# Retention and SwiGLU block: the FFN products by one level of Strassen, over segments of two sequences

## The chip, the cores and the metric

The kernel runs on one core of a Trainium2 chip. The metric is device time in microseconds (us) of one execution; lower is better. One execution was also recorded by the hardware profiler, and all rows below come from that one.

## What is computed

A recurrent retention layer over four sequences of 768 positions, with eight heads of 64, and then a SwiGLU feed-forward block over all 3072 tokens (the model dimension is 512, the inner one 1536):

```python
for t in range(S):
    state = gamma * state + einsum('bhd,bhe->bhde', k[:, :, t], v[:, :, t])
    y[:, :, t] = scale * einsum('bhd,bhde->bhe', q[:, :, t], state)
x = y.transpose(0, 2, 1, 3).reshape(B * S, H * D)     # 3072 x 512
g = x @ w_gate
out = (g / (1 + exp(-g)) * (x @ w_val)) @ w_out
```

`q`, `k`, `v` are float32. The three weight matrices come as float64; the kernel turns them into float32 on the chip.

## The kernel before

Retention is done in chunks of 128 positions, 24 of them, in three steps: `scores` (L175, masked on VectorE at L180, with `qd` and `kd` made on GpSimd at L185 and L189), `mix` (L226 and L230; ScalarE copies the result into `xT` at L233) and `state` (L202, then VectorE at L208 to L212). A chunk's `mix` needs the state that the chunk before it in its sequence left.

The FFN runs over six tiles of 512 tokens. `up` takes one block of 128 of the 1536 inner columns: four float32 matmuls of 128 x 512 for gate and four for value (L257), the Silu on ScalarE (L261) and the product on VectorE (L263). There are twelve such units in a tile. `down` makes 128 tokens of output in twelve matmuls (L268), copied out by ScalarE (L271) and stored; there are four in a tile. All weights lie in SBUF for the whole run. The order is written out by hand in program order: the retention steps of a tile stand between the units of the tile before, so every engine and queue takes its work in that order.

The weights come in 36 pieces of 128 x 512 float64 (12 of gate, 12 of value, 12 of out). A piece is loaded as raw words by a DMA from SP (L107, four raw buffers, three pieces ahead) and turned into float32 in `convert_piece`: six operations on VectorE (L122 to L131), one on ScalarE (L132) and two on GpSimd (L133, L135). Three pieces are converted after each unit of the first tile, four in the prologue.

Of the kernel before, what the change touches and what calls it, by code (L numbers as in the profile page):

```python
# [10 lines left out]
F32 = mybir.dt.float32  # L11
U32 = mybir.dt.uint32
# [13 lines left out]
NT = B * S // T  # L26

# columns of the table of decays
# [5 lines left out]
def tile_retnet_swiglu(  # L34
    ctx: ExitStack,
    tc: tile.TileContext,
    q_t: bass.AP,        # [chunk, (head of pair, d), pair, position]
    k_t: bass.AP,        # likewise
    k_n: bass.AP,        # [chunk, position, (head, d)]
    v_n: bass.AP,        # likewise  # L40
    decays: bass.AP,     # [P, NTAB]
    w_gate: bass.AP,     # float32, or float64 as the bits of int64
# [15 lines left out]
    loads = ctx.enter_context(tc.tile_pool(name="loads", bufs=4))  # L58
    raws = ctx.enter_context(tc.tile_pool(name="raws", bufs=4))
    mid = ctx.enter_context(tc.tile_pool(name="mid", bufs=2))  # L60
    hp = ctx.enter_context(tc.tile_pool(name="hp", bufs=NF + 2))
    io = ctx.enter_context(tc.tile_pool(name="io", bufs=2))
    psum = ctx.enter_context(
        tc.tile_pool(name="psum", bufs=1, space=bass.MemoryType.PSUM))
    ctx.enter_context(tc.manual_schedule())
# [5 lines left out]
    chunks = {}  # L71

    def load_chunk(c):
        tiles = []
        for nm, src in (("kt", k_t), ("qt", q_t), ("kn", k_n), ("vn", v_n)):
            t = loads.tile([P, 512], F32, tag=nm, name=f"{nm}_{c}")
            nc.sync.dma_start(out=t, in_=src[c])
            tiles.append(t)
        chunks[c] = tiles

    tab = consts.tile([P, NTAB], F32, name="tab")
    load_chunk(0)
    nc.scalar.dma_start(out=tab, in_=decays)
    for c in range(1, CPT):
        load_chunk(c)
    wg = [consts.tile([P, NC, P], F32, name=f"wg{f}") for f in range(NF)]
    wv = [consts.tile([P, NC, P], F32, name=f"wv{f}") for f in range(NF)]
    wo = [consts.tile([P, DM], F32, name=f"wo{f}") for f in range(NF)]
    pieces = []
    for f in range(NF):  # L90
        for w, src in ((wg, w_gate), (wv, w_val)):
            pieces.append((w[f].rearrange("p c f -> p (c f)"),
                           src[:, ts(f, P)].rearrange("(c p) f -> p c f", p=P)))
    for f in range(NF):
        pieces.append((wo[f], w_out[ts(f, P)]))
    landed = {}

    def load_piece(n):
        dst, src = pieces[n]
# [10 lines left out]
    def convert_piece(n):  # L110
        """float64 -> float32, rounded to nearest. The words are (lo, hi); hi holds
        the sign, 11 bits of exponent and 20 of mantissa. hi << 3 without its sign is
        the float32 of those 20 bits but for the top bit of the exponent, which is the
        other way round. hi is first brought into float32's range by its magnitude,
        compared as float32 (the order of the bits): below it becomes 0, above inf."""
        if n not in landed:
            return
        dst = pieces[n][0]
# [3 lines left out]
        nc.vector.tensor_scalar(d, hi, 0x7FFFFFFF, None, op0=ALU.bitwise_and)  # L122
# [8 lines left out]
        nc.vector.tensor_scalar(hi, d, 0xFF800000, None, op0=ALU.bitwise_and)  # L131
        nc.scalar.activation(lo.bitcast(F32), lo, AF.Copy, scale=2.0 ** -52)  # L132
        nc.gpsimd.tensor_tensor(lo.bitcast(F32), lo.bitcast(F32), hi.bitcast(F32),  # L133
                                op=ALU.mult)
        nc.gpsimd.tensor_tensor(dst, dst, lo.bitcast(F32), op=ALU.add)  # L135

    AHEAD = 3              # raw pieces on their way
    n_piece = [0]

    def next_piece():  # L140
        n = n_piece[0]
        if n == len(pieces):
            return
        n_piece[0] += 1
        if n + AHEAD < len(pieces):
            load_piece(n + AHEAD)
        convert_piece(n)

    for n in range(AHEAD):
        load_piece(n)  # L150
# [6 lines left out]
    # two states by turns: a pair's two heads as the diagonal blocks of 128 x 128  # L157
    states = [consts.tile([P, NP, P], F32, name=f"state{i}") for i in range(2)]
    for t in states:
        nc.gpsimd.memset(t, 0.0)  # L160

# [1 line left out]
    xT = {}  # L163
    att = {}

    def pairs(t):
        return t.rearrange("p (n t) -> p n t", n=NP)

    def scores(c):
# [13 lines left out]
        if c % NCK:  # L183
            qd = mid.tile([P, NP, P], F32, tag="qd", name=f"qd_{c}")
            nc.gpsimd.tensor_tensor(qd, qt, qdec, op=ALU.mult)  # L185
            att[c, "qd"] = qd
        if c % NCK < NCK - 1:
            kd = mid.tile([P, H, D], F32, tag="kd", name=f"kd_{c}")
# [5 lines left out]
    def state(c):  # L194
# [9 lines left out]
        new, old = states[c % 2], states[(c + 1) % 2]  # L204
# [10 lines left out]
    def mix(c):  # L215
        ci, t, j = c % NCK, c // CPT, c % CPT
        vn = chunks[c][3]
        a = att.pop(c)
        if j == 0:
            xT[t] = mid.tile([P, NC, T], F32, tag="xT", name=f"xT_{t}")  # L220
        y = bank("y", 1, f"y_{c}")
        if ci:
            qd = att.pop((c, "qd"))
            prev = states[(c + 1) % 2]
# [8 lines left out]
        nc.scalar.copy(xT[t][:, :, ts(j, P)], pairs(y))  # L233

    def retention(t):
# [3 lines left out]
        def last(c):  # L239
            state(c)  # L240
            if c + CPT < B * NCK:
                load_chunk(c + CPT)

        steps = []
        for c in range(CPT * t, CPT * (t + 1)):
            steps += [lambda c=c: scores(c), lambda c=c: mix(c), lambda c=c: last(c)]
        return steps

# [1 line left out]
    hT = {}  # L250

    def up(t, f):
        ps = []
        for w in (wg, wv):
            p_ = bank("mlp", 4, f"up{len(ps)}_{t}_{f}")
            for c in range(NC):
                nc.tensor.matmul(p_, w[f][:, c], xT[t][:, c],  # L257
                                 start=(c == 0), stop=(c == NC - 1))
            ps.append(p_)
        sg = io.tile([P, T], F32, tag="sg", name=f"sg_{t}_{f}")  # L260
        nc.scalar.activation(sg, ps[0], AF.Silu)  # L261
        hT[f] = hp.tile([P, T], F32, tag="h", name=f"h_{t}_{f}")
        nc.vector.tensor_tensor(hT[f], sg, ps[1], op=ALU.mult)  # L263

    def down(t, j):
        o = bank("mlp", 4, f"o_{t}_{j}")
        for f in range(NF):
            nc.tensor.matmul(o, hT[f][:, ts(j, P)], wo[f],  # L268
                             start=(f == 0), stop=(f == NF - 1))
        ev = io.tile([P, DM], F32, tag="ev", name=f"ev_{t}_{j}")  # L270
# [77 lines left out]
```

## Time and profile before

| what | value |
|---|---|
| time, median of three runs (lowest, highest) | 964.25 us (964.19, 964.88) |
| span of the profiled execution, first to last instruction | 962.0 us |
| TensorE busy | 861.0 us, 89% of the span |
| VectorE busy | 258.7 us, 27% |
| GpSimd busy | 135.3 us, 14% |
| ScalarE busy | 95.9 us, 10% |
| mean granted TensorE clock | 0.954 of 2.4 GHz |

The span is 2.25 us under the median of the runs. The rows further down come from views of the trace: stretches of time with the busy time of each engine, the waits by what ended them, the chain of work that ended last, the order in time, and groups of like instructions. PE is TensorE, PEld its weight loads, DVE VectorE, ACT ScalarE, POOL GpSimd, and SP the engine whose queue issues most DMAs. A float32 matmul stands in the trace as two records, and some records are missing.

### The profile page before, as it was taken

The page shows a single profiled execution, that of the slowest core. Times are in us where ns is not written, and L with a number is a line of the kernel's source. Part 1 is how long each engine was busy: PE and PEld are TensorE (multiplying, and loading weights), DVE is VectorE, ACT ScalarE, POOL GpSimd, SP SyncE. Part 2 cuts the span into 40 slices and gives each one's busy share as a digit, 9 for nine tenths or more (in the row PEclk, how much of TensorE's full clock was granted, in tenths as well). Part 3 has the DMA queues.
Part 4 walks back from the last instruction along what each step waited for, and adds up shares of the span by engine and source line. Part 5 has one row for each costly group of instructions (what it writes and reads, how often), then busy time and mean ns, then how long its engine had stood idle before and what let it go on. Part 6 is the DMA issues. An engine that isn't in the chain of part 4 may idle for free.

```text
span 962.0 us, 7015 instructions
## 1 busy us (share of the span) xinstructions
PE 861.0 (89%) x2816; PEld 421.7 (44%) x2816; DVE 258.7 (27%) x408; ACT 95.9 (10%) x158; POOL 135.3 (14%) x118
## 2 busy tenths in 40 slices
PE   4797560629999999999999999999999999999998
PEld 3632220314545544444554544444454444444443
DVE  3789999470111211011121012010021210010100
ACT  1121111100000010000000010000000000000000
POOL 2545555360000000000000000000000000000000
PEclk8799985769999999999999999999999999999999
DMA  8223346322120100110111111011000000000000
GB/s 295 86 69 115 124 154 197 110 87 65 48 74 12 45 33 30 58 44 24 32 38 50 33 44 45 11 44 55 33 1 1 0 1 22 22 1 0 0 12 33
DMA packets 31857, 51.58 MB, mean 54 GB/s; under 512 B 2512, under 2 KB 14800, under 8 KB 31824
## 3 DMA queue, kind: packets, MB, share of 16 engines
q1 hardware_dynamic: 28224, 44.05, 14.3%
q10 hardware_dynamic: 3600, 7.09, 2.1%
q8 instruction: 22, 0.36, 0.2%
q14 instruction: 11, 0.09, 0.0%
HBM read 44.83 MB, written 6.29 MB: 53 GB/s over the span
## 4 chain that ended last, share of the span: by engine, by line
PE 77%; DVE 0%; ACT 0%; issue 0%
PE up L257 44%; PE o L268 26%; PE y L230 2%; PE s L175 2%; PE y L226 2%; PE st L202 1%; DVE a L180 0%; ACT ev L271 0%
## 5 line engine op out<-in xcount | busy, mean ns | idle before, releaser
L257 PE MATMUL up<-xT,wv 128*128 128x512 f32 x576 | 266.0, 605 | 20.3 <-DVE h L263 18.1
L257 PE MATMUL up<-xT,wg 128*128 128x512 f32 x576 | 262.1, 598 | 2.6 <-POOL wg L135 2.6
L268 PE MATMUL o<-wo,h 128*128 128x512 f32 x576 | 251.3, 594 | 0.0
L257 PEld LDWEIGHTS up<-xT,wv 128*128 128x128 f32 x576 | 111.4, 195 | 164.2 <-issue 159.6
L263 DVE TENSOR_TENSOR h<-sg,up 128x512 f32<-128x512 f32 x72 | 49.5, 687 | 496.4 <-PE up L257 496.4
L268 PEld LDWEIGHTS o<-wo,h 128*128 128x128 f32 x576 | 108.4, 190 | 133.1 <-issue 132.6
L257 PEld LDWEIGHTS up<-xT,wg 128*128 128x128 f32 x576 | 106.1, 190 | 126.3 <-issue 119.5
L261 ACT ACTIVATE sg<-up 128x512 f32<-128x512 f32 x72 | 42.9, 595 | 366.0 <-PE up L257 366.0
L226 PE MATMUL y<-qd,state 128*128 128x128 f32 x160 | 25.3, 309 | 60.0 <-POOL qd L185 59.4
L185 POOL TENSOR_TENSOR qd<-qt,tab 128x512 f32<-128x512 f32 x20 | 26.0, 1300 | 293.2 <-PE y L226 271.2
L226 PEld LDWEIGHTS y<-qd,state 128*128 128x128 f32 x160 | 23.8, 219 | 67.8 <-POOL qd L185 60.3
L133 POOL TENSOR_TENSOR raw<-raw 128x512 f32<-128x512 f32 x36 | 38.7, 1076 | 104.7 <-issue 89.8
L180 DVE TENSOR_TENSOR a<-s,tab 128x512 f32<-128x512 f32 x48 | 30.9, 686 | 76.5 <-PE s L175 76.4
L189 POOL TENSOR_TENSOR kd<-kn,tab 128x512 f32<-128x512 f32 x20 | 21.4, 1069 | 207.6 <-PE st L202 201.9
L175 PE MATMUL s<-qt,kt 64*128 64x128 f32 x384 | 32.0, 306 | 13.5 <-DMA qt<-in_q_t_dram 6.8
L271 ACT COPY ev<-o 128x512 f32<-128x512 f32 x24 | 14.1, 586 | 262.6 <-PE o L268 262.6
L175 PEld LDWEIGHTS s<-qt,kt 64*128 64x128 f32 x384 | 26.9, 206 | 29.6 <-issue 18.3
L125 DVE TENSOR_SCALAR raw<-raw 128x512 uint32<-128x512 uint32 x36 | 38.8, 1077 | 0.0
L132 ACT ACTIVATE raw<-raw 128x512 f32<-128x512 uint32 x36 | 23.8, 673 | 107.1 <-DMA raw<-in_w_gate_dram 45.4
L230 PE MATMUL y<-a,vn 128*64 128x128 f32 x384 | 31.1, 308 | 1.0 <-issue 0.8
L212 DVE TENSOR_TENSOR state<-state,st 64x256 f32<-64x256 f32 x32 | 13.4, 418 | 61.8 <-PE st L202 60.1
L230 PEld LDWEIGHTS y<-a,vn 128*64 128x64 f32 x384 | 24.4, 155 | 6.1 <-issue 3.6
(30 smaller groups left out, 248.5 us busy)
## 6 DMA issues: line engine op xcount, KB each, us to landing
kt<-in_k_t_dram SPq DMA_DIRECT2D x24, 256.0 KB, 2.8
qt<-in_q_t_dram SPq DMA_DIRECT2D x24, 256.0 KB, 3.3
kn<-in_k_n_dram SPq DMA_DIRECT2D x24, 256.0 KB, 3.6
vn<-in_v_n_dram SPq DMA_DIRECT2D x24, 256.0 KB, 2.8
raw<-in_w_gate_dram SPq DMA_DIRECT2D x12, 512.0 KB, 3.5
raw<-in_w_val_dram SPq DMA_DIRECT2D x12, 512.0 KB, 3.6
raw<-in_w_out_dram SPq DMA_DIRECT2D x12, 512.0 KB, 3.7
out_dram<-ev ACTq DMA_DIRECT2D x24, 256.0 KB, 2.1
```

The costliest lines, as they stand in the source:

```text
L125: nc.vector.tensor_scalar(hi, hi, 0x80000000, None, op0=ALU.bitwise_and)
L132: nc.scalar.activation(lo.bitcast(F32), lo, AF.Copy, scale=2.0 ** -52)
L133: nc.gpsimd.tensor_tensor(lo.bitcast(F32), lo.bitcast(F32), hi.bitcast(F32), op=ALU.mult)
L175: nc.tensor.matmul(sp[i][:, ts(n, P)], kt[r, n], qt[r, n], start=True, stop=True, skip_group_check=True)
L180: nc.vector.tensor_tensor(t, pairs(sp[i]), mask[:, i], op=ALU.mult)
L185: nc.gpsimd.tensor_tensor(qd, qt, qdec, op=ALU.mult)
L226: nc.tensor.matmul(y[:, ts(n, P)], prev[:, n], qd[:, n], start=(n == 0), stop=False, skip_group_check=True)
L230: nc.tensor.matmul(y[ds(D * i, D), ts(n, P)], vn[:, ts(2 * n + i, D)], a[i][:, n], start=(ci == 0 and n == 0), stop=True, skip_group_check ...
L257: nc.tensor.matmul(p_, w[f][:, c], xT[t][:, c], start=(c == 0), stop=(c == NC - 1))
L261: nc.scalar.activation(sg, ps[0], AF.Silu)
L263: nc.vector.tensor_tensor(hT[f], sg, ps[1], op=ALU.mult)
L268: nc.tensor.matmul(o, hT[f][:, ts(j, P)], wo[f], start=(f == 0), stop=(f == NF - 1))
```

## The change

The up and down products of the FFN are computed block-wise by one level of Strassen's method (in Winograd's form): each product of 2 x 2 blocks takes seven block products instead of eight, with additions ahead of them (sums of operands) and behind them (sums of results). The two block rows of the moving side are the tokens of two sequences, 384 of each, so a segment has 768 tokens and there are four segments. For up the two block columns are gate and value; the inner halves are 256 of the 512 model dimensions. For down they are the two halves of 256 output columns and of 768 inner dimensions.

Up (`up`, one unit per block of 128 inner columns, twelve in a segment) has seven products of two matmuls of 128 x 384. They run through the banks `x` and `wz`, two of each, and are accumulated in place: ScalarE copies partial sums out between products (`p1`, `p5`, `u2`), VectorE adds (`hT`, `c11`) and multiplies. Down (one per 128 positions of both sequences, three in a segment) has seven products of six matmuls of 128 x 256. The sums of activations are made on VectorE (`sums_x` before a segment's up, `sum_h` before and within down). The four sums of weight blocks per operand are made on GpSimd (`sums_t`), once.

A weight operand with its sums (`wt`, seven blocks of 128 x 256, 896 KB) no longer stays in SBUF: a ring holds three. In the first segment each is made, used, and stored to DRAM (`wstore`); in the three later segments it is read back two units ahead. The operands of down (`wot`) stay in SBUF.

The conversion of a piece has four VectorE operations, one of ScalarE (with a bias) and one integer addition on GpSimd. It is issued in two halves between the products of the first segment's up units, three pieces to a unit; six pieces are converted in the prologue. There are two raw buffers instead of four. The retention of the first segment (six chunks, the two sequences by turns) runs in the prologue; that of the next segment is issued one step after each product of down. `qd` and `kd` have one buffer each, and there are four states.

The core of the diff:

```diff
-T = 512                # tokens of an FFN tile
-CPT = T // P           # chunks of an FFN tile
+L = 3
+TH = L * P
+NSEG = B * NCK // (2 * L)
-        nc.vector.tensor_scalar(dst, dst, 122880.0, 2.0 ** -15,
-                                op0=ALU.min, op1=ALU.max)
-        nc.vector.tensor_scalar(hi, hi, 0x80000000, None, op0=ALU.bitwise_and)
-        nc.vector.tensor_scalar(d, d, 3, 0x7FFFFFFF,
-                                op0=ALU.logical_shift_left, op1=ALU.bitwise_and)
-        nc.vector.scalar_tensor_tensor(d, d, 0x40000000, hi,
-                                       op0=ALU.bitwise_xor, op1=ALU.bitwise_or)
...
+        def first_():
+            nc.scalar.activation(lo.bitcast(F32), lo, AF.Copy, scale=2.0 ** -51,
+                                 bias=2.0)
+            nc.vector.tensor_scalar(d, hi, 0x7FFFFFFF, None, op0=ALU.bitwise_and)
+            nc.vector.tensor_scalar(dst, dst, 122879.9921875, 2.0 ** -15,
+                                    op0=ALU.min, op1=ALU.max)
+
+        def second():
+            nc.vector.tensor_scalar(hi, hi, 0x80000000, None, op0=ALU.bitwise_and)
+            nc.vector.scalar_tensor_tensor(d, d, 3, hi, op0=ALU.logical_shift_left,
+                                           op1=ALU.bitwise_xor)
+            nc.gpsimd.tensor_tensor(dst.bitcast(I32), dst.bitcast(I32),
+                                    lo.bitcast(I32), op=ALU.add)
...
+        for o, a, b in ((t3, b22, t1), (t1, t1, b11), (t2, b22, t1), (t4, b21, t2)):
+            nc.gpsimd.tensor_tensor(o, a, b, op=ALU.subtract)
...
+    def up(s, f, fill):
...
+        product(x, 0, a_up(0, 0))
+        p1 = tmp("p1")
+        nc.scalar.copy(p1, x)
+        product(wb, 2, s1)
+        p5 = tmp("p5")
+        nc.scalar.copy(p5, wb)
+        fill(2)
+        product(x, 5, s2, start=False)
+        u2 = tmp("u2")
+        nc.scalar.copy(u2, x)
+        fill(2)
+        product(wb, 3, s4, start=False)
+        tt(hT[:, f, 0], wb, u2, op=add)
+        product(x, 4, s3, start=False)
+        tt(hT[:, f, 1], x, p5, op=add)
+        z = bank("wz", 2, f"z_{s}_{f}")[:, :TH]
+        product(z, 1, a_up(0, 1))
+        c11 = tmp("c11")
+        tt(c11, z, p1, op=add)
+        nc.scalar.activation(c11, c11, AF.Silu)
+        fill(1)
+        product(x, 6, a_up(1, 1), start=False)
...
+    for s in range(NSEG):
+        nxt = seg_chunks(s + 1) if s + 1 < NSEG else []
         for f in range(NF):
+            if s:
+                if f + 2 < NF:
+                    kept_wt(s, f + 2)
+            w = wt[s, f]
+            up(s, f, fill if s == 0 else lambda k: None)
+            if s == 0:
+                nc.sync.dma_start(out=wstore[f], in_=w)
```

Here is how the rows stand on the engines. The SP queue in the first tile before: raw loads in a row (`raw` is a raw buffer; the names in brackets are the queues and engines that a row waits for):

```order
L107 DMA raw_221<-in_w_gate_dram 128x4x256 [waits DMAHW1_49,DMAHW5_49,DVE_49,Pool_49]
L107 DMA raw_273<-in_w_val_dram 128x4x256 [waits DMAHW2_49,DMAHW6_49,DVE_49,Pool_49]
L107 DMA raw_325<-in_w_gate_dram 128x4x256 [waits DMAHW3_49,DMAHW7_49,DVE_49,Pool_49]
L107 DMA raw_373<-in_w_val_dram 128x4x256 [waits DMAHW0_49,DMAHW4_49,DVE_49,Pool_49]
L107 DMA raw_384<-in_w_gate_dram 128x4x256 [waits DMAHW5_49,DVE_49,Pool_49]
```

The same queue now, in the first segment's units 0 and 1 (`wstore_84` is the DRAM place of unit 0's operand, `wt_0_140` that operand):

```order
L133 DMA raw_499<-in_w_gate_dram 128x4x256 [waits DMAHW2_49,DMAHW0_49,Pool_49]
L133 DMA raw_528<-in_w_val_dram 128x4x256 [waits DMAHW1_49,Pool_49]
L487 DMA wstore_84<-wt_0_140 128x1792
L133 DMA raw_548<-in_w_out_dram 128x1024 [waits DMAHW2_49,Pool_49]
L133 DMA raw_561<-in_w_gate_dram 128x4x256 [waits DMAHW3_49,Pool_49]
L133 DMA raw_590<-in_w_val_dram 128x4x256 [waits DMAHW5_49,Pool_49]
L487 DMA wstore_85<-wt_1_381 128x1792
```

After every three raw loads there is now a store of an operand, which stands behind the load ahead of it and so behind that load's wait for GpSimd (Pool).

VectorE in the first tile before, at the end of the first unit's work (`h` is the unit's result, `wg_114` the float32 weights that a piece fills):

```order
L263 TENSOR_TENSOR h_0_371<-sg_0_369,up_0_0_364 128x512 [waits PE_49,Activation_49]
L122 TENSOR_SCALAR wg_114<-raw_221 128x512 [waits DMAHW5_49]
L123 TENSOR_SCALAR wg_114<-wg_114 128x512 [waits DVE_49]
L125 TENSOR_SCALAR raw_221<-raw_221 128x512 [waits Pool_49]
L126 TENSOR_SCALAR wg_114<-wg_114 128x512 [waits DVE_49]
L128 SCALAR_TENSOR_TENSOR wg_114<-wg_114,raw_221 128x512 [waits DVE_49]
L131 TENSOR_SCALAR raw_221<-wg_114 128x512 [waits DVE_49]
```

VectorE now, in unit 1 of the first segment (`wt_3_498` is the operand of unit 3, in the ring's place of unit 0):

```order
L153 TENSOR_SCALAR wt_3_498<-raw_499 128x512 [waits DMAHW4_49,DMAHW2_49,PE_49]
L154 TENSOR_SCALAR wt_3_498<-wt_3_498 128x512 [waits DVE_49]
L158 TENSOR_SCALAR raw_499<-raw_499 128x512 [waits Pool_49]
L159 SCALAR_TENSOR_TENSOR wt_3_498<-wt_3_498,raw_499 128x512 [waits DVE_49]
L153 TENSOR_SCALAR wt_3_498<-raw_528 128x512 [waits DMAHW3_49]
L154 TENSOR_SCALAR wt_3_498<-wt_3_498 128x512 [waits DVE_49]
L158 TENSOR_SCALAR raw_528<-raw_528 128x512 [waits Pool_49]
L159 SCALAR_TENSOR_TENSOR wt_3_498<-wt_3_498,raw_528 128x512 [waits DVE_49]
L379 TENSOR_TENSOR hT<-w_1_533,u_0_1_552 128x384 [waits PE_49,Activation_49]
L381 TENSOR_TENSOR hT<-x_1_532,p_0_1_540 128x384 [waits PE_49]
L385 TENSOR_TENSOR c_0_1_576<-z_1_573,p_0_1_536 128x384 [waits PE_49]
```

Four operations make a piece instead of six; the first write of an operand now waits for two DMAs (the raw piece, and the store that empties the place) and for TensorE; and the additions that empty the unit's banks stand behind two pieces.

## Rows read from the trace of the kernel before

**Rows 1.** Stretches of time: us, busy us of each engine (records), clock, DMA, GB/s.
```profile
core 0: us, PE busy (x) PEld busy (x) DVE busy (x) ACT busy (x) POOL busy (x), PEclk, DMA share, GB/s
...
96.00:120.00 24.00, 14.10 (x29) 5.78 (x29) 23.49 (x34) 3.86 (x6) 13.01 (x11) 0.92 0.39 126
...
144.00:168.00 24.00, 0.00 (x0) 0.00 (x0) 23.49 (x34) 3.67 (x6) 12.65 (x11) 0.50 0.61 197
...
192.00:216.00 24.00, 6.86 (x33) 4.11 (x32) 19.18 (x31) 1.84 (x3) 14.95 (x13) 0.70 0.25 80
...
240.00:264.00 24.00, 24.00 (x90) 12.07 (x90) 2.46 (x5) 1.20 (x3) 1.63 (x2) 1.00 0.14 46
...
400.00:600.00 200.00, 200.00 (x665) 96.72 (x664) 28.02 (x47) 17.21 (x29) 10.29 (x9) 1.00 0.12 39
```

**Rows 2.** TensorE's longest waits: us in total, times, longest us.
```profile
PE y L226 <- POOL qd L185: 59.4, 4, 37.7
PE up L257 <- DVE h L263: 18.1, 4, 5.0
```

**Rows 3.** The chain that ended last, in order of time: start us, us, what.
```profile
371.32 10.30 PE o L268 x24
...
510.32 10.30 PE o L268 x24
...
834.69 82.40 PE up L257 x192
917.09 41.22 PE o L268 x96
```

**Rows 4.** TensorE in order of time: short matmuls between long ones, at full clock.
```profile
363.40 1.05 PE L202 MATMUL st<-vn,kd 128*128 128x128 f32 x8
364.29 3.60 PE L257 MATMUL up<-xT,wg 128*128 128x512 f32 x8
```

**Rows 5.** Groups by line and shape: busy us, mean ns; VectorE's conversion of gate pieces.
```profile
L125 DVE TENSOR_SCALAR raw<-raw 128x512 uint32<-128x512 uint32 x36 | 38.8, 1077 | 0.0
...
L123 DVE TENSOR_SCALAR wg<-wg 128x512 f32<-128x512 f32 x12 | 12.3, 1028 | 0.4
L128 DVE SCALAR_TENSOR_TENSOR wg<-wg,raw 128x512 uint32<-128x512 uint32 x12 | 8.3, 692 | 0.4
...
L122 DVE TENSOR_SCALAR wg<-raw 128x512 uint32<-128x512 uint32 x12 | 6.9, 575 | 7.6 <-DMA raw<-in_w_gate_dram 7.6
...
L131 DVE TENSOR_SCALAR raw<-wg 128x512 uint32<-128x512 uint32 x12 | 5.2, 429 | 0.4
...
L126 DVE TENSOR_SCALAR wg<-wg 128x512 uint32<-128x512 uint32 x12 | 5.0, 416 | 0.0
```

**Rows 6.** VectorE in order of time, the first piece, while GpSimd has nothing to do.
```profile
17.73 0.43 DVE L122 TENSOR_SCALAR wg<-raw 128x512 uint32<-128x512 uint32 x1 [7.59 <-DMA raw<-in_w_gate_dram]
...
19.33 0.69 DVE L128 SCALAR_TENSOR_TENSOR wg<-wg,raw 128x512 uint32<-128x512 uint32 x1
```

**Rows 7.** Groups by line and shape: elementwise work of other lengths, and GpSimd's addition.
```profile
L263 DVE TENSOR_TENSOR h<-sg,up 128x512 f32<-128x512 f32 x72 | 49.5, 687 | 496.4 <-PE up L257 496.4
...
L211 DVE TENSOR_TENSOR state<-state,tab 64x256 f32<-64x256 f32 x32 | 18.0, 563 | 0.2
...
L135 POOL TENSOR_TENSOR wg<-wg,raw 128x512 f32<-128x512 f32 x12 | 16.3, 1356 | 0.9
...
L212 DVE TENSOR_TENSOR state<-state,st 64x256 f32<-64x256 f32 x32 | 13.4, 418 | 61.8 <-PE st L202 60.1
```

**Rows 8.** DMA issues by line: count, KB each, median us from issue to landing.
```profile
raw<-in_w_out_dram SPq DMA_DIRECT2D x12, 512.0 KB, 3.7
out_dram<-ev ACTq DMA_DIRECT2D x24, 256.0 KB, 2.1
tab<-in_decays_dram ACTq DMA_DIRECT2D x1, 774.0 KB, 5.3
```

**Rows 9.** The prologue in order of time: the first raw piece, and the last chunk's state.
```profile
17.73 0.69 ACT L132 ACTIVATE raw<-raw 128x512 f32<-128x512 uint32 x1 [15.27 <-DMA raw<-in_w_gate_dram]
...
43.37 1.68 PE L202 MATMUL st<-vn,kd 128*128 128x128 f32 x8
```

More of the change, by code (lines that the diff above doesn't have):

```diff
@@ L11 @@
 F32 = mybir.dt.float32
+I32 = mybir.dt.int32
 U32 = mybir.dt.uint32
@@ L131, in convert_piece @@
[L131 to L147, printed above, removed]
@@ new lines, in tile_retnet_swiglu, with place @@
+    down_pieces = []
+    for j in range(FH):
+        for i in range(2):
+            down_pieces.append((j, i, w_out[ts(j + FH * i, P)]))
+    order = []
+    for f in range(NF):
+        order += [("up",) + pieces[2 * f], ("up",) + pieces[2 * f + 1]]
+        order.append(("down",) + down_pieces[f])
+    def place(n):
+        kind, a, i, _ = order[n]
+        if kind == "up":
+            w = wt[0, a] if (0, a) in wt else new_wt(0, a)
+        else:
+            w = wot[a]
+        return w, w[:, ds(2 * i, 2)].rearrange("p a b -> p (a b)")
@@ new lines, in tile_retnet_swiglu, with load_next, steps_of_piece, after @@
+    AHEAD = 2
+    n_loaded = [0]
+    def load_next():
+        n = n_loaded[0]
+        if n < len(order):
+            n_loaded[0] += 1
+            load_piece(n, place(n)[1], order[n][3])
+    def steps_of_piece(n):
+        kind, a, i, _ = order[n]
+        def after():
+            for s in todo[n]:
+                s()
+            load_next()
+            if i == 1:
+                sums_t(place(n)[0], 2 if kind == "up" else 1)
+        todo = {}
+        def one():
+            steps = convert_piece(n, place(n)[1])
+            todo[n] = steps[1:]
+            for s in steps[:1]:
+                s()
+        return [one, after]
@@ L232, in mix @@
                                  skip_group_check=True)
[L233 to L246, printed above, removed]
-        return steps
[L250 to L263, printed above, removed]
@@ L282, in tile_retnet_swiglu @@
[L282 to L297 removed]
+        nc.scalar.copy(xT[:, :, c // NCK % 2, ts(ci % L, P)], pairs(y))
@@ new lines, in retention, with last @@
+    def retention(s):
+        cs = seg_chunks(s)
+        def last(n):
+            state(cs[n])
+            del chunks[cs[n]]
+            if s and n + 2 < len(cs):
+                load_chunk(cs[n + 2], loads, "")
+        steps = [lambda: scores(cs[0])]
+        for n, c in enumerate(cs):
+            if n + 1 < len(cs):
+                steps.append(lambda n=n: scores(cs[n + 1]))
+            steps.append(lambda c=c: mix(c))
+            steps.append(lambda n=n: last(n))
+        return steps
@@ new lines, in down, with product, tmp, more @@
+    def down(s, u, step):
+        x = bank("x", 2, f"dx_{s}_{u}")[:, :DH]
+        wb = bank("wz", 2, f"dw_{s}_{u}")[:, :DH]
+        cur = dict(hs)
+        def product(o, slot, a, start=True):
+            for k in range(FH):
+                nc.tensor.matmul(o, a[:, k], wot[k][:, slot], start=(start and k == 0),
+                                 stop=(k == FH - 1), skip_group_check=True)
+            step()
+        def tmp(nm):
+            return io.tile([P, TH], F32, tag=nm, name=f"d{nm}_{s}_{u}")[:, :DH]
+        def more(*ns):
+            for n in ns:
+                if u + 1 < L:
+                    sum_h(n, u + 1)
+        ev = [io.tile([P, DM], F32, tag=f"ev{i}", name=f"ev{i}_{s}_{u}", bufs=1)
+              for i in range(2)]
+        tt = nc.vector.tensor_tensor
+        product(x, 0, a_dn(0, 0, u))
+        p1 = tmp("p1")
+        nc.scalar.copy(p1, x)
+        product(wb, 1, cur[1])
+        p5 = tmp("p5")
+        nc.scalar.copy(p5, wb)
+        product(x, 5, cur[2], start=False)
+        u2 = tmp("u2")
+        nc.scalar.copy(u2, x)
+        product(wb, 3, cur[4], start=False)
+        tt(ev[0][:, DH:], wb, u2, op=ALU.add)
+        more(1, 2, 4)
+        product(x, 4, cur[3], start=False)
+        tt(ev[1][:, DH:], x, p5, op=ALU.add)
+        more(3)
+        z = bank("wz", 2, f"dz_{s}_{u}")[:, :DH]
+        product(z, 2, a_dn(0, 1, u))
+        tt(ev[0][:, :DH], z, p1, op=ALU.add)
+        product(x, 6, a_dn(1, 1, u), start=False)
+        nc.scalar.copy(ev[1][:, :DH], x)
+        p, pos = divmod(s * L, NCK)
+        for i in range(2):
+            row = (2 * p + i) * S + (pos + u) * P
+            nc.scalar.dma_start(out=out[ds(row, P)], in_=ev[i])
@@ new lines, in tile_retnet_swiglu @@
+    cs = seg_chunks(0)
+    load_chunk(cs[0], first, "0")
+    nc.scalar.dma_start(out=tab, in_=decays)
+    for n in range(1, len(cs)):
+        load_chunk(cs[n], first, str(n))
+        if n == 2:
+            for _ in range(AHEAD):
+                load_next()
+    steps = retention(0)
+    for n, st in enumerate(steps):
+        st()
+        if n >= 8 and n % 2 == 0 and len(fillers) > 2 * (len(order) - 6):
+            fill(1)
+    fill(len(fillers) - 2 * (len(order) - 6))
+    sums_x()
+    early.__exit__(None, None, None)
@@ new lines, in tile_retnet_swiglu, with step @@
+    hp = ctx.enter_context(tc.tile_pool(name="hp", bufs=1))
+    hT = hp.tile([P, NF, 2, TH], F32, name="hT")
+    for s in range(NSEG):
+        nxt = seg_chunks(s + 1) if s + 1 < NSEG else []
+        for f in range(NF):
+            if s:
[5 more added lines that the diff above has]
+                nc.sync.dma_start(out=wstore[f], in_=w)
+        for c in nxt[:2]:
+            load_chunk(c, loads, "")
+        for n in (1, 2, 4, 3):
+            sum_h(n, 0)
+        steps = retention(s + 1) if nxt else []
+        def step():
+            if steps:
+                steps.pop(0)()
+        for u in range(L):
+            if u == 1 and nxt:
+                kept_wt(s + 1, 0)
+                kept_wt(s + 1, 1)
+            down(s, u, step)
+        while steps:
+            steps.pop(0)()
+        if nxt:
+            sums_x()
```

153 lines of the change are left out of this document (89 added, 64 removed).

## The prediction, made before the changed kernel was run

> **What bounds the kernel now.** I read the windows first. From 240 us on TensorE is busy in every window at a granted clock of 1.00, and the other engines are far from full; before that it loses time: 14.10 of 24 us busy at 96 to 120, none at 144 to 168, 6.86 at 192 to 216, while VectorE is at 23.5 of 24 us through the first two [rows 1]. So there are two stages with two limits. In the first, the float64 weights are turned into float32 on VectorE, and the waits name what TensorE misses: 59.4 us for GpSimd's `qd`, which stands in GpSimd's queue behind the conversions, and 18.1 us for VectorE's `h` [rows 2]. In the second only the matmuls count.
>
> The second stage has exact prices. The last tile runs without retention: 192 records (two for each float32 matmul of 512 columns) in 82.40 us and 96 in 41.22 us, so 429.2 ns a record [rows 3], which is 2 x 512 columns at 2.4 GHz (426.7 ns) and 2.5 ns on top. A tile with the retention of four chunks takes 510.32 - 371.32 = 139.0 us [rows 3], so a chunk costs (139.0 - 82.4 - 41.2) / 4 = 3.85 us. Six tiles and 24 chunks are 741.7 + 92.4 = 834 us; the tail after the last matmul is 962.0 - 958.3 = 3.7; so about 124 us of the span are lost in the first stage. The change touches both stages, so I work out both.
>
> **Matmuls.** A block of 768 tokens (2 x 384) takes seven products where eight stood. Up: 4 segments x 12 units x 7 products x 2 = 672 matmuls of 384 columns. Down: 4 x 3 x 7 x 6 = 504 of 256 columns. With the same 2.5 ns on top a record is 322.5 or 215.8 ns, so a matmul is 645 or 432 ns: 433.4 + 217.6 = 651.0 us against 741.7, a gain of 91 us. Does each record still hide the load of its weights when it is this short? Before, the shortest full one has 128 columns: eight records of `st` start at 363.40 and the next product at 364.29, so 111 ns each [rows 4], 2 ns over the 109 that the same rule gives. Loads are hidden there, and I take them as hidden at 256 and 384. The bound on the other side is the record's whole length with its drain, 1.05 us / 8 = 131 ns, 22 ns more a record: +52 us over 2352 records.
>
> The page "TensorE: Matmul & The Clock Gate" of the Trainium skill (Back-to-back issue gap) says that in a stream of weight loads and matmuls the two set the spacing together, some 81 ns at 128 columns against 56 alone. As an estimate from that page, 25 ns a pass and 50 ns a record would add 118 us here and make the kernel slower. The 111 ns record speaks against it; it is the last rival below.
>
> **The seven products' additions in the later segments.** An up unit has 9.03 us of matmuls. VectorE adds five operations of 384 columns; between 418 ns at 256 and 687 ns at 512 columns that is 0.55 us each, 0.74 with both operands in SBUF (563 against 418) [rows 7], so some 3.2 us. ScalarE has five of less than 0.6 us. Each bank that is read between two products has one other product (1.29 us) for it, against some 0.2 us of drain and 0.55 us of reading. In down one other product is 2.6 us, with retention steps between products. VectorE's operand sums of 768 columns (about 1 us each) lie there too: 12 per segment, and four more ahead of the next segment, started while the last product runs. I see no engine near its limit, and charge 0 to 8 us for the seams, taken as 2. The kept weights come back with 896 KB per 9 us unit, two units ahead; the slowest landing of such a size in the trace is 5.3 us [rows 8], so the loads are covered. If they weren't, each microsecond late would cost 36 us over the 36 reloaded units.
>
> **The first segment.** Its up units must wait for converted weights, so the chain there is VectorE's. A piece drops two short VectorE operations (416 and 429 ns) and one of GpSimd's two; four remain, 575 + 1028 + 1077 + 692 ns = 3.37 us [rows 5]. That mean holds waiting for GpSimd: the same work began at 17.73 us and ended 1.97 us of busy time later where GpSimd was idle (0.43 + 0.43 + 0.42 + 0.69; its first and last rows in [rows 6]). GpSimd's new load per piece is one addition (of integers, which the trace doesn't have; the float one is 1.36 us [rows 7]; half or twice that would move a unit by 0.7 or 1.4 us) and two or three half-length subtractions. That is like the old load, so I keep 3.37 where it works and 1.97 where it is idle.
>
> Units 0 to 9 each convert three pieces, for the unit two ahead and for down. VectorE then has 3 x 3.37 + 3 x 0.55 + 0.74 = 12.5 us against 9.0 of TensorE: VectorE bound. From unit 1 on there is a new wait. The ring has three places, so the first write of unit f+2's weights needs the place of unit f-1, and that needs its store to DRAM to have landed. The order of SP puts this store behind a raw load that waits for GpSimd's addition in the last piece of unit f-1. So from VectorE's last step of one unit to its first of the next there are: GpSimd 1.36, SP and signals 0.1, then the store. No store of 896 KB is in the trace. A 256 KB store lands in 2.1 us and a 774 KB load beside others in 5.3 [rows 8]; the line through both gives 6.0 us, counted from the raw load just ahead. The bounds are 0 (landed before it is asked for) and 9.7 (a 512 KB raw load's 3.7 and the 6.0 one after the other). I take 6.0: link 7.5 us. What is queued behind VectorE's waiting operation are the two pieces and the three additions that empty the banks; TensorE waits for those before its last product of the unit, so all of the link shows.
>
> A unit is then 1.97 (GpSimd idle after the link) + 2 x 3.37 + 1.65 + 0.74 + 7.5 = 18.6 us. Behind the last converted piece TensorE still has one product and two units, 19.4 us, and some 2 us at the lower clock, less the 4.7 us by which its release comes before that piece's end: +16.7.
>
> **The prologue.** Six chunks, six pieces and four operand sums come ahead of unit 0. Before, four chunks and four pieces end at 43.37 + 1.68 = 45.05 us [rows 9]. Two more chunks on VectorE (3.3 us each), two more pieces (6.7), the sums (3.8) less the removed operations (4 x 0.85) give 58.7. Before, VectorE also sat idle until the first raw piece at 17.73 [rows 9]; the new order has retention work for half of that. I take 55 (48 to 65). Retention of segment 0 is paid here, and GpSimd's `qd` no longer stands behind conversions later.
>
> **Sum.** 55 + 12.5 (unit 0) + 9 x 18.6 + 16.7 = 251.6 us at the end of up 0. Down 0 with six chunks: 126 x 0.432 + 6 x 3.85 = 77.5. Segments 1 and 2: 108.4 + 54.4 + 23.1 = 185.9 each. Segment 3: 162.8. Tail 3.7, seams 2. Together 869.4 us of span. The profiled run's span of 962.0 stands 2.25 us under the median of 964.25; with that 871.6, so 871 us, about 10% faster. The first stage then loses about as much as now (869 - 651 - 92 - 4 = 122 us): the gain is the matmuls'.
>
> **Rivals.**
> 1. The store has landed by the time that its place is wanted, or the wait hides. The unit falls to VectorE's 12.5 us, 9 x 6.1 = 55 us less: 816. For it: the transfer alone is short (2.1 us for 256 KB). Against it: SP issues it only after the unit's last addition.
> 2. The first segment is heavier: the store at its upper bound (+3.7 us a unit), or TensorE at its lower clock most of the time, since it idles half of each unit. The granted clock was 0.50 in the idle window and 0.70 where it worked a little [rows 1]; seven products at 1.2 GHz are 18 us, about the unit itself. 3.7 x 9 = +33: 904.
> 3. Slower: the shorter matmuls show their weight loads. From 93 us / 2352 = 40 ns a record on, the change loses; at 50 ns it is 871 + 118 = 989. Row against it: 111 ns at 128 columns.
>
> **How the numbers follow.** Forecast 0.50, rival 1 0.20, rival 2 0.24, rival 3 0.04; 0.02 for a time close to before. What a measurement here can tell from no change is about 0.2%. The cases from 820 (a store that mostly hides) to 915 (rival 2 and a slow prologue) hold some 8 in 10. Faster 0.95, same 0.01, slower 0.04.
>
> **What would show it.** Up units of the later segments at 9.0 us, with records of 322 and 216 ns; a VectorE that stands still 6 to 8 us before the first write of each `wt` in units 1 to 9, released by the `wstore` DMA; up of the first segment ending near 250 us. A first segment that ends by 200 us is rival 1, one near 285 rival 2; a unit of over 9.6 us in the later segments is rival 3. Gaps over 1 us between products in later segments would make the seams wrong.

## The result, and the profile after

The changed kernel takes 879.33 us (median of four runs, 879.09 to 880.69) against 964.22 (962.71 to 964.88) for the one before: a ratio of 0.9127, 95% interval 0.9114 to 0.9140. The forecast was 871 us with a range of 820 to 915. The profiled execution took 879.36 us, with a span of 877.6.

The first view is stretches of time, with the columns of [rows 1]: the prologue, units 1 to 9 of the first segment, then the up and the down of the second segment.

```profile
0.00:60.00 60.00, 36.43 (x283) 28.93 (x284) 40.42 (x60) 9.98 (x16) 32.42 (x35) 0.81 0.54 189
...
72.00:241.00 169.00, 101.46 (x249) 56.02 (x248) 90.74 (x151) 38.76 (x71) 77.33 (x79) 0.77 0.41 137
...
337.49:445.85 108.36, 108.36 (x337) 63.84 (x337) 33.99 (x61) 29.24 (x60) 1.04 (x1) 1.00 0.29 101
445.85:524.20 78.35, 78.35 (x525) 67.36 (x525) 36.75 (x58) 7.70 (x18) 10.79 (x9) 1.00 0.30 103
```

There are two stages with two limits again. In the up and the down of the second segment TensorE is busy all of the time, at a granted clock of 1.00. In the first segment it works 101 of 169 us at 0.77, and no other engine is full either: VectorE has 91. Something there is a latency, not an engine. The chain of work that ended last, which the trace follows back to 224.94 us, names it (start us, us, what):

```profile
225.39 5.92 DMA wstore<-wt
...
237.31 5.03 PE x L359 x8
...
259.11 2.59 PE dx L418 x12
262.80 2.79 PE dw L418 x12
...
345.23 2.58 PE x L359 x8
...
354.26 2.58 PE x L359 x8
...
819.32 2.59 PE dx L418 x12
821.91 2.59 PE dw L418 x12
...
873.75 0.37 ACT ev L452
```

Behind the store that empties an operand's place come VectorE's conversions and additions, and from 237.31 us on there is only TensorE, up to the last copy. In the later segments a unit of up is 354.26 - 345.23 = 9.03 us, and a product of down without retention 821.91 - 819.32 = 2.59 us for twelve records. Up 0 ends where down's first product starts, at 259.11.

How a unit of the first segment goes is read from VectorE, GpSimd and SP in order of time (start, us, engine, line, operation; in brackets the idle time before it and what ended it):

```profile
65.75 0.56 DVE L379 TENSOR_TENSOR hT<-w,u 128x384 f32<-128x384 f32 x1
...
98.53 0.43 DVE L153 TENSOR_SCALAR wt<-raw 128x512 uint32<-128x512 uint32 x1 [7.07 <-PE z L359]
...
100.70 1.28 POOL L161 TENSOR_TENSOR wt<-wt,raw 128x512 int32<-128x512 int32 x1 [4.88 <-DVE wt L159]
100.86 1.41 DVE L154 TENSOR_SCALAR wt<-wt 128x512 f32<-128x512 f32 x1
...
109.33 0.55 DVE L393 TENSOR_TENSOR hT<-hT,sg 128x384 f32<-128x384 f32 x1
...
109.54 1.48 POOL L161 TENSOR_TENSOR wot<-wot,raw 128x512 int32<-128x512 int32 x1 [1.15 <-DVE wot L159]
...
111.05 0.38 SPq L133 DMA_DIRECT2D raw<-in_w_val_dram  x1
...
111.48 0.50 SPq L487 DMA_DIRECT2D wstore<-wt  x1
...
117.51 0.43 DVE L153 TENSOR_SCALAR wt<-raw 128x512 uint32<-128x512 uint32 x1 [7.63 <-DMA wstore<-wt]
...
217.14 0.55 DVE L379 TENSOR_TENSOR hT<-w,u 128x384 f32<-128x384 f32 x1
```

From 98.53 VectorE works 10.8 us, to its last multiplication at 109.33. GpSimd then adds the last piece's low words, SP issues the raw load that waited for that, and only behind it the store. VectorE stands still for 7.63 us until the store has landed. From unit 0's first addition (65.75) to unit 8's (217.14) a unit takes 18.92 us.

Nine units have such a wait, and the trace doesn't put all of them down to the store (group by line and shape: busy us, mean ns, then the idle time before it by what ended it):

```profile
L153 DVE TENSOR_SCALAR wt<-raw 128x512 uint32<-128x512 uint32 x24 | 11.2, 466 | 70.5 <-DMA wstore<-wt 38.3 <-issue 15.2 <-PE z L359 14.7
```

Five of the nine (38.3 us) are put down to the store; two are given to TensorE's `z`, as the one at 98.53, and two to nothing that the profile shows. Whether they are all one wait is for experiment 1 to decide.

### The profile page after: what moved, and what is told of

Read it like the earlier page. It is cut to its first block, busy times and chain, and to the rows that moved or that the text cites. A ratio compares the mean times of both kernels' runs of the same rounds, so it can differ in the third digit from the quotient of the medians.

```text
span 877.6 us, 8898 instructions
## 1 busy us (share of the span) xinstructions
PE 780.5 (89%) x3440; PEld 542.7 (62%) x3440; DVE 372.9 (42%) x604; ACT 173.3 (20%) x350; POOL 158.1 (18%) x156
## 4 chain that ended last, share of the span: by engine, by line
PE 73%; DMA 1%; DVE 1%; issue 0%; SPq 0%; ACT 0%; DVEq 0%
PE x L359 23%; PE dx L418 15%; PE w L359 11%; PE dw L418 7%; PE z L359 6%; PE dz L418 4%; PE s L261 2%; PE y L314 2%; PE y L310 2%; PE st L288 1%; DMA wstore<-wt 1%; DVE wt L154 0%; DVE wt L153 0%; DVE wt L159 0%; DVE raw L158 0%
## 5 line engine op out<-in xcount | busy, mean ns | idle before, releaser
L359 PE MATMUL x<-xT,wt 128*128 128x384 f32 x384 | 155.6, 554 | 69.6 <-DVE hT L381 69.6
L359 PEld LDWEIGHTS x<-xT,wt 128*128 128x128 f32 x384 | 82.3, 218 | 132.4 <-issue 91.4
L359 PE MATMUL w<-xs,wt 128*128 128x384 f32 x384 | 141.6, 492 | 13.1 <-DVE xs L346 13.1
L359 PE MATMUL x<-xs,wt 128*128 128x384 f32 x384 | 140.9, 490 | 0.0
L359 PEld LDWEIGHTS w<-xs,wt 128*128 128x128 f32 x384 | 74.6, 195 | 67.2 <-POOL wt L170 14.5
L359 PEld LDWEIGHTS x<-xs,wt 128*128 128x128 f32 x384 | 73.5, 191 | 51.6 <-issue 1.2
L359 PE MATMUL z<-xT,wt 128*128 128x384 f32 x192 | 69.8, 486 | 0.0
L418 PE MATMUL dw<-wot,hs 128*128 128x256 f32 x288 | 67.6, 384 | 0.0
L418 PE MATMUL dx<-wot,hs 128*128 128x256 f32 x288 | 67.0, 382 | 0.0
L418 PE MATMUL dx<-wot,hT 128*128 128x256 f32 x288 | 66.4, 381 | 0.0
L161 POOL TENSOR_TENSOR wt<-wt,raw 128x512 int32<-128x512 int32 x24 | 31.2, 1298 | 86.7 <-DVE wt L159 60.2
```

What stands on the lines that cost most here:

```text
L161: nc.gpsimd.tensor_tensor(dst.bitcast(I32), dst.bitcast(I32), lo.bitcast(I32), op=ALU.add)
L359: nc.tensor.matmul(o, w[:, slot, k], a[:, k], start=(start and k == 0), stop=(stop and k == KH - 1), skip_group_check=True)
L418: nc.tensor.matmul(o, a[:, k], wot[k][:, slot], start=(start and k == 0), stop=(k == FH - 1), skip_group_check=True)
```

## Experiments

Changes are against the changed kernel, unless said otherwise. "Unit" is the mean from unit 0's first addition to unit 8's.

**1. The store ahead of its unit.** The operand is ready before its unit begins, so its store need not stand behind the unit's raw loads.

```diff
             w = wt[s, f]
-            up(s, f, fill if s == 0 else lambda k: None)
             if s == 0:
                 nc.sync.dma_start(out=wstore[f], in_=w)
+            up(s, f, fill if s == 0 else lambda k: None)
```

> The store of a unit's operand is issued at the unit's start, one unit earlier in SP's order; nothing else changes. Theory A (the store's landing holds the first segment): the 8.2 us between VectorE's last step of a unit and the next first write go, but with two raw buffers the second piece's raw load then ends last (issued after the last addition, landing about 6.2 us after VectorE's last step), so the unit falls from 19.0 to about 15 us and the time by 9 x 4 = 36 us, to 840 to 848. Theory B (conversion on VectorE and GpSimd is the limit and the wait only stands in its place): within 10 us of the changed kernel, 870 to 880.

Measured: 835.46 us (832.84 to 835.62), ratio 0.8665 (0.8651 to 0.8679). That is 44 us less than the changed kernel, a little better than the first account's range; a unit takes 14.12 us. All nine long waits go, those that the trace had not put down to the store too. Two rows from the list of this kernel's waits (engine, line, what ended them: us in total, times, longest):

```profile
PE x L359 <- DVE hT L381: 30.8, 10, 4.9
...
DVE wt L153 <- DMA raw<-in_w_val_dram: 20.2, 10, 2.6
```

The first stood at 69.6 us in ten waits in the changed kernel. Of VectorE's wait of 7.6 us some 2 are left, and another transfer ends them: a raw piece, which has only two buffers.

**2. A third raw buffer, alone.** (The `sg` tile gets one buffer for it, so that all fits.)

```diff
-    raws = ctx.enter_context(tc.tile_pool(name="raws", bufs=2))
+    raws = ctx.enter_context(tc.tile_pool(name="raws", bufs=3))
-    AHEAD = 2
+    AHEAD = 3
-        sg = tmp("sg")
+        sg = io.tile([P, TH], F32, tag="sg", name=f"sg_{s}_{f}", bufs=1)
```

> Three raw buffers and three pieces ahead, the store where it was. Theory A: the store still ends last, so units stay at 19 us; only the prologue's waits for raw pieces (2 to 4 us) go: 873 to 880. Theory C (raw loads, not the store, bind the first segment): 25 to 40 us less.

Measured: 875.43 us (874.70 to 876.63), ratio 0.9080 (0.9067 to 0.9094), 4 us less. An earlier raw piece is worth little as long as the store is what the operand waits for:

```profile
DVE wt L153 <- DMA wstore<-wt: 39.3, 5, 8.0
```

**3. Both.**

> Store at the unit's start and three raw buffers. Theory A: with both waits gone a unit is VectorE's own work, 11 to 12 us instead of 19, so 9 x 7 to 8 us and a few us of the prologue go: 800 to 820. Theory B: 860 to 880. Theory C: the same as with three raw buffers alone.

Measured: 819.72 us (819.12 to 820.27), ratio 0.8501 (0.8488 to 0.8514). Together 60 us, more than 44 + 4: the second wait could only go when the first was gone. Up 0 ends at 199.84. A unit takes 12.91 us, more than the 11 to 12 expected, and the time lies at the upper edge of the first account's range. The stretch from unit 0's first addition to unit 8's shows who is the limit now (columns as above):

```profile
63.93:167.21 103.28, 82.76 (x224) 46.20 (x224) 101.14 (x137) 33.33 (x64) 73.26 (x72) 0.90 0.61 193
```

VectorE, 101.1 of 103.3 us. This is the case that the prediction had as rival 1 (816 us, 12.5 us a unit); it took two edits.

**4. The eighth product put back.** The product into `z` is made twice, in up and in down; all else stays.

```diff
         product(z, 1, a_up(0, 1))
+        product(z, 1, a_up(0, 1))
...
+        for k in range(FH):
+            nc.tensor.matmul(z, a_dn(0, 1, u)[:, k], wot[k][:, 2], start=(k == 0),
+                             stop=(k == FH - 1), skip_group_check=True)
         product(z, 2, a_dn(0, 1, u))
```

> An eighth product: the z product of each up unit and of each down block is made twice into the same bank, so the matmul work is that of the plain block product while all else stays. If the later segments are bound by matmuls alone, it costs 36 x 1.29 + 12 x 2.59 + 2 x 1.29 = 80 us, with the first segment's other ten units hiding theirs under the store: 955 to 965. If another engine set the pace of the later segments, less: under 930.

Measured: 960.54 us (959.81 to 961.39), ratio 0.9962 (0.9947 to 0.9977), 81.2 us more. By the records the eighth product is 48 x 1.29 + 12 x 2.59 = 93.0 us. In the first segment TensorE waits anyway: down 0 starts at 262.06 instead of 259.11, so 2.95 of its 12 x 1.29 = 15.5 us show and 12.5 are hidden, which leaves 80.5. A unit of the later segments in its chain is 364.97 - 354.65 = 10.32 us, 1.29 more than without it:

```profile
262.06 2.59 PE dx L419 x12
...
354.65 2.58 PE z L359 x8
...
364.97 2.58 PE z L359 x8
```

**5. The old conversion in the changed kernel.** Six operations of VectorE and two of GpSimd for a piece.

```diff
-            nc.scalar.activation(lo.bitcast(F32), lo, AF.Copy, scale=2.0 ** -51,
-                                 bias=2.0)
+            nc.scalar.activation(lo.bitcast(F32), lo, AF.Copy, scale=2.0 ** -52)
...
-            nc.vector.scalar_tensor_tensor(d, d, 3, hi, op0=ALU.logical_shift_left,
-                                           op1=ALU.bitwise_xor)
-            nc.gpsimd.tensor_tensor(dst.bitcast(I32), dst.bitcast(I32),
-                                    lo.bitcast(I32), op=ALU.add)
+            nc.vector.tensor_scalar(d, d, 3, 0x7FFFFFFF,
+                                    op0=ALU.logical_shift_left, op1=ALU.bitwise_and)
+            nc.vector.scalar_tensor_tensor(d, d, 0x40000000, hi,
+                                           op0=ALU.bitwise_xor, op1=ALU.bitwise_or)
+            nc.vector.tensor_scalar(hi, d, 0xFF800000, None, op0=ALU.bitwise_and)
+            nc.gpsimd.tensor_tensor(lo.bitcast(F32), lo.bitcast(F32), hi.bitcast(F32),
+                                    op=ALU.mult)
+            nc.gpsimd.tensor_tensor(dst, dst, lo.bitcast(F32), op=ALU.add)
```

> The changed kernel with the old conversion (six VectorE operations and two on GpSimd a piece). Theory A, in which VectorE's work of a unit and the store's wait add up: two operations of 0.42 us more on VectorE, one of 1.08 us more on GpSimd that also stretches VectorE's, so 2.5 to 5.5 us a unit on ten units and 5 to 9 us in the prologue: 910 to 945. Rival (conversion was no part of the gain): within 8 us of the changed kernel, 875 to 887.

Measured: 935.34 us (935.13 to 935.65), ratio 0.9704 (0.9688 to 0.9720). One store, and the wait that it ends, in order of time:

```profile
134.30 0.50 SPq L490 DMA_DIRECT2D wstore<-wt  x1
...
140.51 0.43 DVE L152 TENSOR_SCALAR wt<-raw 128x512 uint32<-128x512 uint32 x1 [8.94 <-DMA wstore<-wt]
```

A unit is 24.1 us instead of 18.9: the added work of the three pieces lies in the chain from store to store, and VectorE's wait at its end, which begins with GpSimd's work on the last piece, grows from 7.6 to 8.9. Down 0 starts at 315.01, 55.9 us later than at 259.11: all of the 56 us lie ahead of it, in the prologue and the first segment's up.

**6. The new conversion in the kernel before,** and nothing else of the change (the edit above, the other way round).

> The kernel before with the new conversion alone. Before, a piece takes VectorE 4.46 us in the first tile; with four operations and one wait for GpSimd it should take about 3.2, so 32 pieces give back some 40 us: 915 to 930. The conversion then holds about half of the whole gain when made alone. Rival (the retention's place in GpSimd's queue, not the conversion, sets the first stage): 950 to 965.

Measured: 910.02 us (909.13 to 910.52), ratio 0.9439 (0.9425 to 0.9454): a gain of 54 us, above what I expected (34 to 49). The waits of [rows 2] in this kernel, and two of the stretches around the place of [rows 1] in which TensorE stood still:

```profile
PE y L222 <- POOL qd L181: 33.7, 2, 23.9
...
PE up L253 <- DVE h L259: 1.8, 1, 1.8
```

```profile
144.00:168.00 24.00, 14.25 (x60) 8.29 (x59) 13.74 (x23) 2.45 (x4) 12.19 (x10) 0.72 0.34 110
168.00:192.00 24.00, 23.03 (x80) 10.88 (x80) 1.98 (x3) 1.77 (x3) 0.00 (x0) 1.00 0.13 44
```

The two waits fall from 77.5 us to 35.5, which is 42. The rest is found in the totals of this execution (busy us, and as a share of its span of 908.5 us):

```profile
PE 853.5 (94%) x2816; PEld 419.7 (46%) x2816; DVE 206.2 (23%) x336; ACT 96.2 (11%) x158; POOL 95.7 (11%) x82
```

Before, TensorE was busy for 861.0 of 962.0 us. So its idle time falls by 101.0 - 55.0 = 46 us, and the same matmuls take 7.5 us less, at a mean granted clock of 0.972 instead of 0.954: it came back to full clock earlier, 1.00 from 168 us on, where the kernel before had 0.70 at 192 to 216.

The four kernels make a table:

| | old conversion | new conversion |
|---|---|---|
| eight products, weights in SBUF | 964 | 910 |
| seven products, weights through DRAM | 935 | 879 |

The conversion gives 54 or 56 us, the rest of the change 29 or 31. The two add up to within 2 us.

**7. On 3: the operand sums taken from GpSimd.** To see what GpSimd's sums cost VectorE, they are left out and ScalarE copies three blocks in their place.

```diff
-        for o, a, b in ((t3, b22, t1), (t1, t1, b11), (t2, b22, t1), (t4, b21, t2)):
-            nc.gpsimd.tensor_tensor(o, a, b, op=ALU.subtract)
+        for o, a in ((t3, b22), (t2, b11), (t4, b21)):
+            nc.scalar.copy(o, a)
```

> On the version with the store at the unit's start and three raw buffers: GpSimd's four subtractions per operand are left out, and ScalarE copies three blocks into the places of the sums (so the products are not those of the reference). Theory A2 (VectorE's 12.9 us unit is 8.7 us of its own work and 4 us of standing behind GpSimd): units fall to 10 to 11 us, 793 to 803. Rival (VectorE's own work alone): 815 to 822.

Measured: 810.80 us (809.69 to 811.80), ratio 0.8411 (0.8398 to 0.8423), between the two ranges; a unit takes 11.68 us. The first two rows are groups of VectorE by line in experiment 3, from unit 0's first addition to unit 8's; the next rows are the same groups here, then the stretch and a wait of ScalarE:

```profile
L389 DVE TENSOR_TENSOR hT<-hT,c 128x384 f32<-128x384 f32 x8 | 8.6, 1075 | 0.0
...
L379 DVE TENSOR_TENSOR hT<-w,u 128x384 f32<-128x384 f32 x9 | 5.0, 552 | 0.0
```

```profile
L379 DVE TENSOR_TENSOR hT<-w,u 128x384 f32<-128x384 f32 x9 | 5.0, 552 | 3.0 <-PE w L359 3.0
L389 DVE TENSOR_TENSOR hT<-hT,c 128x384 f32<-128x384 f32 x8 | 4.4, 556 | 4.7 <-ACT c L386 4.7
```

```profile
58.94:152.35 93.41, 78.61 (x221) 43.36 (x220) 79.98 (x137) 44.70 (x101) 34.80 (x25) 0.95 0.66 215
```

```profile
ACT wt L170 <- POOL wt L161: 45.6, 12, 7.2
```

The sums do stretch VectorE: the same multiplication falls from 1075 to 556 ns. VectorE's busy time for a unit falls from 101.14 / 8 = 12.6 to 79.98 / 8 = 10.0 us. But of these 2.6 us a unit only 1.2 reach the end: VectorE now waits for TensorE's products and for ScalarE, whose copies stand in its queue until GpSimd's integer addition is done. So it is shown that GpSimd's sums lengthen VectorE's work; what the whole of that costs the kernel's time isn't, since the replacement brought a wait of its own. Sums that block no other queue were not tried.

**8. On 3: the pieces of down later.** In 3 VectorE is full in units 0 to 9 and has nothing to convert in 10 and 11, and two pieces of down's weights are converted ahead of unit 0. Here the prologue and units 0 and 1 convert none of them, and units 10 and 11 two each.

```diff
         order += [("up",) + pieces[2 * f], ("up",) + pieces[2 * f + 1]]
-        order.append(("down",) + down_pieces[f])
+        if f >= 4:
+            order.append(("down",) + down_pieces[f - 4])
+    order += [("down",) + d for d in down_pieces[NF - 4:]]
...
-            up(s, f, fill if s == 0 else lambda k: None)
+            left = [4 if f < 2 or f > 9 else 6]
+
+            def some(k):
+                k = min(k, left[0]) if s == 0 else 0
+                left[0] -= k
+                fill(k)
+            up(s, f, some)
```

> On the same version: the conversions of the out pieces are moved later, none in the prologue or in units 0 and 1, two each in units 10 and 11 where VectorE is half idle. Theory A2: two pieces (5.6 us) leave the prologue and two leave units that VectorE bounds (6.6 us): 803 to 812. Rival (units 10 and 11 or down then wait for out weights): 815 to 825.

Measured: 813.87 us (813.50 to 814.56), ratio 0.8444 (0.8431 to 0.8456), 6 us less than 3, between the two ranges: the gain is there, at half the size hoped for. The second product of unit 0 starts 7 us earlier, at 53.12 in 3 and at 46.08 here:

```profile
53.12 2.90 PE L359 MATMUL w<-xs,wt 128*128 128x384 f32 x4 [10.96 <-DVE xs L346]
```

```profile
46.08 2.90 PE L361 MATMUL w<-xs,wt 128*128 128x384 f32 x4 [4.84 <-DVE xs L348]
```

What came off the prologue stays off up to the end of up 0 (near 191 instead of 200), and the step from unit 0 to unit 1 is 9.4 us, near the 9.03 of TensorE's own records. But 2.2 of these 8.7 us are lost again in down 0. VectorE's sums for down (`hs`), 0.96 us each in 3, take up to 1.91 beside GpSimd's `qd` and `kd`, which now stand behind the late pieces, and TensorE waits for a mask product behind them:

```profile
194.00 1.91 DVE L410 TENSOR_TENSOR hs<-hs,hT 128x768 f32<-128x768 f32 x1
```

```profile
199.15 1.75 PE L263 MATMUL s<-qt,kt 64*128 64x128 f32 x16 [1.57 <-DVE a L268]
```

This is the fastest kernel of the study that makes the whole result: 15.6% under the kernel before and 7.4% under the changed one.

## Why the prediction held, point by point

**The later segments** came as worked out. Up is 108.36 us against 108.4 in the sum, records are 1.29 / 4 = 322.5 ns and 2.59 / 12 = 215.8 ns, as 2 x 384 and 2 x 256 columns at 2.4 GHz with the 2.5 ns of [rows 3] give. There are no seams: the 2 us charged for them weren't needed. Down is 78.35 against 77.5: a product with a step of retention behind it often takes 2.79 us instead of 2.59 (the row at 262.80 above), so the chunk's 3.85 us from [rows 3] is (78.35 - 77.5) / 6 = 0.14 too little here.

**Rival 3** is refuted: the 215.8 ns of a 256-column record are the two passes and 2.5 ns, with no room for the weight loads. The Trainium skill's page "TensorE: Matmul & The Clock Gate" (Back-to-back issue gap) has loads and matmuls set the spacing together, 81 ns at 128 columns and 131 at 512. The traces here, with float32, don't agree: a record is as long as two passes over its columns, and half of one is 55.5 ns at 128 columns [rows 4] and 214.6 at 512 [rows 3]. The 989 us was an estimate that carried the page's difference at 128 columns over to 256 and 384, where the section has no such figure. The 111 ns row of `st` [rows 4] was the right one to go by, though it lay one size below. Experiment 4 says the same from the other side: a product costs its records, 1.29 us a unit.

**The link**, the time from VectorE's last step of one unit to its first of the next, was the step that mattered, and it was there: VectorE's wait ended by the store, with what the prediction named ahead of it in SP's queue. It is 117.51 - 109.33 = 8.2 us from VectorE's last operation of one unit to its first of the next, with that operation's own 0.55; the sum had 7.5. The store itself takes 5.9 us where I had drawn a line through two transfers [rows 8] and read 6.0. That it came so near is in part luck, since the line went through a store and a load, and a load of the same 896 KB takes 4.6:

```profile
wt<-wstore SPq DMA_DIRECT2D x36, 896.0 KB, 4.6
wstore<-wt SPq DMA_DIRECT2D x12, 896.0 KB, 5.9
```

VectorE's working part came out at 10.8 us against 11.1. Unit and unit: 18.92 against 18.6. Rival 1 did not come (the store did not hide), and experiments 1 and 3 show by what it would have.

**The prologue** was 5 us short, and it is the largest miss of the sum: unit 0's pieces begin at 60.01, not at 55. VectorE in order of time:

```profile
47.42 0.43 DVE L153 TENSOR_SCALAR wt<-raw 128x512 uint32<-128x512 uint32 x1 [2.18 <-DMA raw<-in_w_val_dram]
...
50.35 0.72 DVE L153 TENSOR_SCALAR wot<-raw 128x512 uint32<-128x512 uint32 x1 [0.97 <-DMA raw<-in_w_out_dram]
...
53.86 1.47 DVE L346 TENSOR_TENSOR xs<-xT 128x768 f32<-128x768 f32 x1
55.36 1.92 DVE L347 TENSOR_TENSOR xs<-xs,xT 128x768 f32<-128x768 f32 x1
...
60.01 0.94 DVE L153 TENSOR_SCALAR wt<-raw 128x512 uint32<-128x512 uint32 x1
```

The prologue of the kernel before, as a stretch:

```profile
0.00:45.05 45.05, 26.40 (x185) 23.04 (x186) 24.39 (x43) 6.97 (x10) 19.39 (x21) 0.77 0.56 193
```

Two terms make it up, each about half. I took an operand sum of 768 columns at its length alone (0.95 us), where beside GpSimd's work it takes up to 1.92; the four take 60.01 - 53.86 = 6.2 us instead of 3.8. And the 3.7 us that I took off, because retention would fill VectorE's idle start, came only to 1.1: VectorE is idle 60.0 - 40.4 = 19.6 us ahead of unit 0, and was idle 45.05 - 24.39 = 20.7 before. Of the 19.6, the two rows show 3.2 of waiting for raw pieces, which have two buffers, and I had no term for that; with three (experiment 2) unit 0's pieces begin at 57.57.

**The sum.** The last converted piece's unit ends on VectorE at 243.05 us against 234.9 in the working: 5.0 from the prologue and 3.1 from nine units. The tail behind it was 16.1 instead of 16.7. So up 0 ends at 259.1 instead of 251.6; three downs with retention add 2.6, and without the seams the span is 877.6 against 869.4. Rival 2, a heavier first segment with 33 us more, lies in that direction, but the units gave only 3; its second half, TensorE at its lower clock, was seen (0.77 in the segment, and 5.03 us for the eight records at 237.31, twice their length at full clock). It cost little, since VectorE and the store set the period: 5.03 - 2.58 = 2.45 us behind the last piece, where the sum had 2.

**What was wrong is the sentence on where the gain comes from.** "The first stage then loses about as much as now (...): the gain is the matmuls'" is true of the sums: 877.6 - 651.0 - 92.4 - 3.7 = 130.5 us are lost now, against 124. As an account of the cause it is half of it. With the old conversion the changed kernel is 56 us slower (experiment 5), with the eighth product 81 (experiment 4): 137 together, where the whole gain is 85. So what came along with the seven products takes some 52 us back, if the two add up, which was not run; with it, the seven products are worth the 29 of the table. I had summed the removed conversion operations and the added link into one unit time and never asked what the unit would be with one of them alone. Where most of the loss lies is shown: moving the store gives back 44 us, and experiment 3 gives back 60 with two edits that change no arithmetic. What the operand sums on GpSimd and the two more pieces and chunks ahead of unit 0 take was not measured by itself.

## What to carry to other kernels

When a change has several parts, work out what each would be worth by itself: two large terms of opposite sign that cancel in one stage look like a stage that was left alone. A transfer that frees a buffer belongs in its queue at the point where its data is ready, not where its data is last used; and before it is moved, look what ends second: here too few raw buffers kept 16 of 60 us until a third was added. An engine that shows 54% busy in a stretch can still be in the chain there, if each of its pauses is ended by a transfer that was issued behind its own work.

## What the runs showed of the hardware

Two things had not been expected. VectorE's operations with one operand from PSUM, where TensorE writes its results, keep their time beside GpSimd (`hT<-w,u`, 552 ns in experiment 3 and in 7, with GpSimd busy 73 of 103 us and 35 of 93). Some operations that read and write SBUF alone are stretched: the bounding of 128 x 512 from 0.43 to 1.41 us (the row at 100.86, beside GpSimd's addition at 100.70), a multiplication of 384 columns from 556 ns in experiment 7 to 1075 in 3. The Trainium skill's page "GPSIMD Engine Reference" (1. Specifications) says that GpSimd shares its SBUF interface with VectorE and contends with VectorE's instructions that have two SBUF inputs or run in a two-port mode. The multiplication, which has two SBUF inputs, agrees; in which mode the bounding ran, no run here shows. Experiments 3 and 7 put the price of GpSimd's sums at 2.6 us of VectorE's time a unit.

And GpSimd's work did not shrink in proportion to its length. From the groups by line and shape of the changed kernel (busy us, mean ns):

```profile
L170 POOL TENSOR_TENSOR wt<-wt 128x256 f32<-128x256 f32 x48 | 39.4, 820 | 3.8
L161 POOL TENSOR_TENSOR wt<-wt,raw 128x512 int32<-128x512 int32 x24 | 31.2, 1298 | 86.7 <-DVE wt L159 60.2 <-issue 17.4 <-DVE wt L153 9.1
```

A subtraction of 256 columns takes 820 ns where the float addition of 512 took 1356 [rows 7]: 60% of the time for half of the length. Both are means beside a working VectorE, so they may hold some waiting. The integer addition of 512 columns, which the trace of before did not have, takes 1298 ns, about what I had taken for it.
